# Staging the first-stage weights in eight places, and moving the token weights' two halves to other points of the queues

## The chip, the cores and the metric

The kernel runs on one core of a Trainium2 chip. The metric is the device time of one execution in microseconds (us), smaller is better. A core has five engines with queues of their own that run in order: TensorE (PE in the profile, with PEld for the loads of its stationary operand), VectorE (DVE), ScalarE (ACT), GpSimd (POOL) and SyncE (SP), which here issues every DMA.

## The reference, cut to what matters

Three layers follow one another, for 4 batches of 576 positions. The part that matters here is the first two:

```python
# layer 1: 8 heads of 64, four with a local band of 32 positions, four with stride 32
attn = softmax(mask(q @ k.T / 8)) @ v              # joined over the heads: x, 576 x 512
# layer 2
theta = x @ w_theta
zr, zi = x * cos(theta), x * sin(theta)
y = einsum('ts,bsd->btd', w_tok_r, zr) + einsum('ts,bsd->btd', w_tok_i, zi)
u = x + y
x = u + maximum(u @ w_ch, 0)
# layer 3: a gate picks 2 of 4 experts for each position; each expert is a causal
# attention of width 64 with projections wq, wk, wv, wo
```

w_theta, w_tok_r, w_tok_i and w_ch (w_theta 512 x 512, w_tok 576 x 576, w_ch 512 x 512) reach the chip as 64-bit floating-point numbers and are turned into 32-bit ones on the core.

## The kernel before, in words

Every product is made of three matmuls (`mm3`): each operand is split into a high and a low part, and high by high, high by low and low by high are summed in PSUM.

**Weights.** `load64` brings in a 64-bit weight in pieces of 128 rows by 256 or 288 columns. A piece is one DMA from SP (line 131) into a place of raw storage in `X[3]`, which is free so early; a cast on ACT of the top 16 bits (line 135); a shift and or on DVE (line 136), which ends the use of the place; and the split into a high part on ACT (line 102) and a low part on DVE (line 104, or line 106 where a scale is applied). `wth` (the angles' weights) has 8 pieces, `wtk` (the tokens' weights) two halves of 9 pieces, `wch` 8 pieces. There are four places; piece c uses place c % 4. The casts' results lie in `X[2]`, also four in number.

**The batches.** `attn_pair(b, pair)` computes one pair of heads of the first layer in three groups: scores into a PSUM tile `s`, exponentials on ACT, sums and reciprocals on DVE, a product with the reciprocal on POOL (line 212), transposes into `tp` (line 215), a copy `pt` (line 219), the product with the values into `av` (line 238), and a copy into `X[b]` (lines 243 and 245). `theta(b, h)` splits `X[b]` (`split_x`, only for h = 0), then forms the angles of one half of the channels in five tiles `th`, reduces them on DVE (lines 283, 284) and takes cosine and sine on ACT (lines 285, 297, 298). `rotate(b, h)` transposes `X[b]` into `xn` (line 305), multiplies it with cosine and sine on DVE (lines 315, 321, 322) and splits the result z (line 327 on ACT or 325; line 329). `tokens(b, h)` multiplies z with `wtk`, the first half of the output positions (n = 0) and then the second (n = 1), and adds into `X[b]` (line 344); `channels(b)` is the product with `wch`.

**The order.** A list scheduler orders each engine's queue from the program's order (which is the priority) and from modelled times; an instruction that is ready in its model may stand before one that comes earlier in the program. `issue_after(ins)` queues each instruction of a block behind `ins` on `ins`'s engine, and only there. For batch 0 the program has: the pairs 0 and 1, `wth`, the pairs 2 and 3; `theta(0, 0)`; the loads of batch 1's pair 0; `rotate(0, 0)`; the first half of `wtk`; `theta(0, 1)`; `rotate(0, 1)`; the second half of `wtk`; batch 1's pairs 0 and 1; `tokens(0, 0)`; `wch`; batch 1's pairs 2 and 3; `tokens(0, 1)`. While the first batch's attention runs (pool `ps0`), and from `theta(0, 0)` on (pool `ps1`), all eight PSUM banks are dealt out: in `ps1` two `acc` (for `th`, `y` and the channels' product), one `xn`, two `s`, one `t`, two `av`.

Of the kernel before, what the change touches and what calls it, by code (L numbers as in the profile page):

```python
# [12 lines left out]
F32 = mybir.dt.float32  # L13
F32R = mybir.dt.float32r
U32 = mybir.dt.uint32
U16 = mybir.dt.uint16
# [3 lines left out]
ALU = mybir.AluOpType  # L20
# [3 lines left out]
B, S, DM, HD, NE = 4, 576, 512, 64, 4  # L24
NT = 5
TW = [128, 128, 128, 128, 64]
HALF = S // 2
# [7 lines left out]
BLK = S // 32  # L35
# [12 lines left out]
def fused_kernel(ctx: ExitStack, tc: tile.TileContext, ql, kl, vl, qs, ks, vs, wth, wtk, wch, wqk, wvg, wo, out):  # L48
    nc = tc.nc

    def f(ap):
        return ap.bitcast(F32)
# [4 lines left out]
    X = [xpool.tile([128, 4, S], F32, name=f"X{b}") for b in range(B)]  # L57
# [27 lines left out]
    for rw in (LQ, RQ):  # L85
        t = wb.tile([128, 2, rw], BF16, name=f"twice{rw}")
# [30 lines left out]
    def new_split(pool, kt, n, name):  # L117
        return tuple(pool.tile([128, kt, n], F32R, name=f"{name}_{part}") for part in ("hi", "lo"))

    def load64(dst, src, kt, n0, n1, scale=1.0):  # L120

        hi, lo = dst
        n = n1 - n0
        for c in range(kt):
            raw = X[3].bitcast(U16)[:, c % 4, :4 * n]
            st = X[2][:, c % 4, HALF:HALF + n]  # L130
            nc.sync.dma_start(raw[:, :4 * n - 1], src[:, c, n0:n1].bitcast(U16)[:, 1:])
            mid = raw.bitcast(U32).rearrange("p (n t) -> p n t", t=2)[:, :, 0]
            top = raw.bitcast(BF16).rearrange("p (n t) -> p n t", t=4)[:, :, 2]
            head = X[2][:, c % 4, :n]
            got = nc.scalar.copy(head.bitcast(F16).rearrange("p (n t) -> p n t", t=2)[:, :, 1], top)
            nc.vector.scalar_tensor_tensor(st.bitcast(U32), mid, 13, head.bitcast(U32), op0=ALU.logical_shift_right,
                                           op1=ALU.bitwise_or)
            split_w(hi[:, c, n0:n1], lo[:, c, n0:n1], st, scale, nc.vector)
        return got.ins
# [2 lines left out]

        return b == 0 and pair != 2 or b == 1 and g == 0

    ps_of, loaded = {}, {}

    def load_pair(b, pair, ain, qbufs, kbufs):
        local = pair < 2
# [78 lines left out]
    def values(b, pair, part, xo, turned):  # L227
        local = pair < 2
        rw, kw = (LQ, LK) if local else (RQ, RQ)
        r0 = part[0][0]  # L230
        av = ps_of[b].tile([128, 512], F32, tag="av", bufs=2, name=f"av_{b}_{pair}_{r0}")
        with tc.issue_after(turned.ins) if b else nullcontext():
            for j0, pt, wd, vg in part:
                for i, wi in enumerate(wd):
                    w = kw if local else wi
                    c0 = rw * (j0 - r0 + i)
                    for h in range(2):
                        nc.tensor.matmul(av[64 * h:64 * h + 64, c0:c0 + wi], vg[:w, i, h, :], pt[:w, i, h, :wi],  # L238
                                         start=True, stop=True)
        c = sum(sum(wd) for _, _, wd, _ in part)  # L240
        copy = nc.scalar.copy if b == 0 else nc.vector.tensor_copy
        if local:
            copy(xo[:, rw * r0:rw * r0 + c], av[:, :c])
        else:
            copy(xo.rearrange("p (t r) -> p r t", r=32)[:, 3 * r0:3 * r0 + c // BLK, :],
                 av[:, :c].rearrange("p (r t) -> p r t", t=BLK))

    def split_act(x, name):
        hi = act.tile([128, S], F32R, tag="ahi", name=f"{name}_hi")
        lo = act.tile([128, S], F32R, tag="alo", name=f"{name}_lo")  # L250
        if len(xsplit) == B:
            nc.scalar.copy(hi, x)
        else:
            nc.vector.tensor_copy(hi, x)  # L254
        eng = nc.vector if not xsplit or len(xsplit) == B and name.endswith(("0", "2")) else nc.gpsimd
        eng.tensor_tensor(lo, x, f(hi), op=ALU.subtract)  # L256
        return hi, lo

    def mm3(ps, ahi, alo, bhi, blo, first, last):
# [7 lines left out]
    sins, turns = {}, {}  # L267
    xsplit, trig, z = {}, {}, {}

    def theta(b, h):  # L270
        if h == 0:
            xsplit[b] = split_x(b)
        xs = xsplit[b]
        d0 = 256 * h
        for t in range(NT):
            w, t0 = TW[t], 128 * t
            th = ps1.tile([128, 512], F32, tag="acc", bufs=2, name=f"th_{b}_{h}_{t}")
            for c in range(4):
                turned = mm3(th[:w, :256], xs[c][0][:, t0:t0 + w], xs[c][1][:, t0:t0 + w],
                             wth_hi[:, c, d0:d0 + 256], wth_lo[:, c, d0:d0 + 256], c == 0, c == 3)  # L280
            cs = rp.tile([128, 2, 256], F32, tag="cs", name=f"cs_{b}_{h}_{t}")
            r = cs[:w, 1, :]
            nc.vector.tensor_scalar_add(r, th[:w, :256], MAGIC)
            nc.vector.scalar_tensor_tensor(r, r, MAGIC, th[:w, :256], op0=ALU.subtract, op1=ALU.subtract)  # L284
            last = nc.scalar.activation(cs[:w, 0, :], r, AF.Abs)
            trig[h, t] = cs
            if b == 0:
                sines(b, h, range(t, t + 1))
        if b > 0:
            with tc.issue_after(last.ins):  # L290
                sines(b, h, range(NT))
        return turned.ins
# [7 lines left out]
    def rotate(b, h):  # L300
        for t in range(NT):
            w, t0, cs = TW[t], 128 * t, trig[h, t]
            xn = ps1.tile([128, 512], F32, tag="xn", bufs=1, name=f"xn_{b}_{h}_{t}")
            for c in range(2):
                nc.tensor.transpose(xn[:w, 128 * c:128 * c + 128], X[b][:, 2 * h + c, t0:t0 + w], ident)
            if t < 4:
                zf = cs
                if h == 0:
                    hi = zu.tile([128, S], F32R, tag="zuhi", name=f"zhi_{b}_{h}_{t}")
                    lo = zu.tile([128, S], F32R, tag="zulo", name=f"zlo_{b}_{h}_{t}")  # L310
                else:
                    hi = z1.tile([128, 512], F32R, tag=f"zhi{t}", name=f"zhi_{b}_{h}_{t}")
                    lo = z1.tile([128, 512], F32R, tag=f"zlo{t}", name=f"zlo_{b}_{h}_{t}")
                hi, lo = (v[:, :512].rearrange("p (a c) -> p a c", a=2) for v in (hi, lo))
                nc.vector.tensor_tensor(zf, cs, xn[:, None, :256].to_broadcast([128, 2, 256]), op=ALU.mult)
                z[h, t], z[h, 4 + t] = (hi[:, 0, :], lo[:, 0, :]), (hi[:, 1, :], lo[:, 1, :])
            else:
                zf = cs[:, 0, :]
                hi = zu.tile([128, 256], F32R, tag="z8hi", bufs=2, name=f"zhi_{b}_{h}_{t}")
                lo = zu.tile([128, 256], F32R, tag="z8lo", bufs=2, name=f"zlo_{b}_{h}_{t}")  # L320
                nc.vector.tensor_tensor(zf[0:64], xn[:64, :256], cs[:64, 0, :], op=ALU.mult)
                nc.vector.tensor_tensor(zf[64:128], xn[:64, :256], cs[:64, 1, :], op=ALU.mult)
                z[h, 8] = (hi, lo)
            if t % 2 == 0 and b > 0:
                nc.vector.tensor_copy(hi, zf)  # L325
            else:
                turns[b, h] = nc.scalar.copy(hi, zf).ins
            eng = nc.gpsimd if b > 0 else nc.vector
            eng.tensor_tensor(lo, zf, f(hi), op=ALU.subtract)  # L329

    us = {}

# [65 lines left out]

    for b in range(B):
        theta(b, 0)  # L400
        if b > 0:
            next_pair(b, 0)
            channels(b - 1)
        else:
            load_pair(1, 0, ain, 2, 2)
        rotate(b, 0)
        if b > 0:
            next_pair(b, 1)
        else:
            load64(wtk_s, wtk, 9, 0, HALF)  # L410
        turned = theta(b, 1)
        if b > 0:
            next_pair(b, 2)
        rotate(b, 1)
        if b == 0:
            load64(wtk_s, wtk, 9, HALF, S)
        if b == B - 1:
            with tc.issue_after(turns[b, 1]):
                nc.scalar.activation(spark, halfpi, AF.Exp)
            pha.close()  # L420
            wc = ctx.enter_context(tc.tile_pool(name="wc", bufs=1, side="right"))
            with tc.tile_pool(name="ws", bufs=3, side="right") as ws:
                with tc.issue_after(turns[b, 1]):
                    wqk_hi, wqk_lo = load_split(wc, ws, wqk, 4, 512, "wqk")
                    wvg_hi, wvg_lo = load_split(wc, ws, wvg, 4, 260, "wvg")
        if b == 0:
            with tc.issue_after(turned), tc.issue_after(sins[0, 1]):
                next_pair(b, 0)
                next_pair(b, 1)
        tokens(b, 0)  # L430
        if b == 0:
            with tc.issue_after(sins[0, 1]):
                for n0 in range(0, DM, 256):
                    load64(wch_s, wch, 4, n0, n0 + 256)
            next_pair(b, 2)
        next_pair(b, 3)
        tokens(b, 1)
# [347 lines left out]
```

## Time and profile before

| what | value |
|---|---|
| median of three runs | 566.6 us (565.12 to 568.58) |
| the profiled execution, its own time | 568.04 us |
| its span in the profile | 566.1 us |
| PE busy, share of the span | 531.6 us, 94% |
| DVE busy | 400.9 us, 71% |
| ACT busy | 317.3 us, 56% |
| POOL busy | 194.8 us, 34% |

The profile shows one execution. Its time is 1.9 us above its span, and 1.4 us above the median of the runs. Busy shares are averages over stages with different limits; the edit concerns the first 140 us.

### The profile page before, as it was taken

Reading aid. Unit: us, or ns where it says so; the run is one execution under the profiler, and the core shown is the slowest. Engines: PE = TensorE matmul, PEld = TensorE weight load, DVE = VectorE, ACT = ScalarE, POOL = GpSimd, SP = SyncE. Lnnn points to the kernel's source line nnn. Section 1 sums busy time; section 2 is a strip of 40 time slices with the busy share of each in tenths; the row PEclk is TensorE's granted clock in tenths of the full one; section 3 lists DMA queues with packets and bytes.
Section 4 is the critical chain, followed back from the end, with each engine's and each line's share of the span. In section 5 each row is a group of like instructions: output and inputs, shape, how many; then the busy total and the mean of one; then the engine's idle time right before and its main releaser. Section 6 shows DMA issues by size and latency. Waiting matters only on the chain.

```text
span 566.1 us, 12493 instructions
## 1 busy us (share of the span) xinstructions
PE 531.6 (94%) x4536; PEld 507.1 (90%) x4536; DVE 400.9 (71%) x1210; ACT 317.3 (56%) x904; POOL 194.8 (34%) x285
## 2 busy tenths in 40 slices
PE   5876799999999999999999999998999999999987
PEld 4855699999899999999999999897989999999987
DVE  3686998576666566856357543588988898888972
ACT  3886894433635226272143450386778668867873
POOL 2210002331265101535104470364455533634451
PEclk9957999999999999999999999999999999999999
DMA  9759341434020213000100020100001001100012
GB/s 268 233 181 316 115 147 52 133 124 156 1 86 23 97 35 117 26 23 8 57 1 1 1 58 0 38 2 2 0 10 45 34 1 33 54 1 12 33 43 85
DMA packets 20389, 37.53 MB, mean 66 GB/s; under 512 B 2904, under 2 KB 12296, under 8 KB 20328
## 3 DMA queue, kind: packets, MB, share of 16 engines
q1 hardware_dynamic: 20328, 36.73, 20.5%
q8 instruction: 36, 0.59, 0.4%
q14 instruction: 25, 0.20, 0.1%
HBM read 32.01 MB, written 4.72 MB: 65 GB/s over the span
## 4 chain that ended last, share of the span: by engine, by line
PE 69%; DVE 14%; DMA 8%; ACT 7%; issue 2%; POOL 1%; SPq 0%; DVEq 0%; POOLq 0%; ACTq 0%
PE y L260 7%; PE y L261 7%; PE y L262 7%; PE s L185 4%; PE th L260 3%; PE av L238 3%; DMA X<-in_wtk 3%; PE th L262 3%; PE th L261 3%; PE tp L617 3%; PE g L260 3%; PE g L261 3%; PE g L262 3%; DVE nm L596 2%; PE tp L215 2%; PE s L591 2%
## 5 line engine op out<-in xcount | busy, mean ns | idle before, releaser
L260 PE MATMUL y<-wtk_hi,zhi 128*128 128x288 f32 x288 | 86.3, 300 | 0.4 <-DVE X L344 0.4
L262 PE MATMUL y<-wtk_hi,zlo 128*128 128x288 f32 x288 | 85.6, 298 | 0.0
L261 PE MATMUL y<-wtk_lo,zhi 128*128 128x288 f32 x288 | 85.6, 297 | 0.0
L212 POOL TENSOR_TENSOR p<-p,sm 128x288 f32<-128x288 f32 (+2 forms) x48 | 28.7, 603 | 157.2 <-DVE sm L211 118.6
L614 POOL TENSOR_SCALAR p<-p,sm,gt 128x256 f32<-128x256 f32 (+1 forms) x64 | 45.2, 710 | 52.1 <-DVE sm L612 34.0
L607 ACT ACTIVATE p<-s,nm 128x128 f32<-128x128 f32 (+2 forms) x96 | 49.5, 518 | 15.0 <-DVE nm L596 7.9
L260 PEld LDWEIGHTS y<-wtk_hi,zhi 128*128 128x128 f32 x288 | 54.1, 188 | 0.7 <-DVE X L344 0.7
L329 POOL TENSOR_TENSOR zlo<-cs,zhi 128x512 fp32r<-128x512 f32 (+1 forms) x30 | 35.8, 1206 | 54.0 <-DVE zhi L325 43.3
L261 PEld LDWEIGHTS y<-wtk_lo,zhi 128*128 128x128 f32 x288 | 54.1, 188 | 0.1
L262 PEld LDWEIGHTS y<-wtk_hi,zlo 128*128 128x128 f32 x288 | 54.0, 188 | 0.1
L260 PE MATMUL th<-wth_hi,x_hi 128*128 128x256 f32 (+1 forms) x160 | 48.1, 301 | 4.9 <-DVE cs L284 3.4
L596 DVE TENSOR_REDUCE nm<-s 128x1 f32<-128x128 f32 (+2 forms) x96 | 44.2, 468 | 5.3 <-PE s L594 4.4
L185 PE MATMUL s<-k,q 128*108 128x54 f32 (+2 forms) x320 | 43.1, 277 | 3.3 <-DMA k<-in_kl 3.3
L261 PE MATMUL th<-wth_lo,x_hi 128*128 128x256 f32 (+1 forms) x160 | 45.9, 288 | 0.0
L262 PE MATMUL th<-wth_hi,x_lo 128*128 128x256 f32 (+1 forms) x160 | 45.7, 289 | 0.0
L185 PEld LDWEIGHTS s<-k,q 128*108 128x108 f32 (+1 forms) x320 | 41.2, 199 | 4.2 <-issue 4.0
L219 ACT COPY pt<-tp 96x384 f32<-96x384 f32 (+2 forms) x44 | 20.9, 477 | 40.8 <-PE tp L215 40.6
L256 POOL TENSOR_TENSOR x_lo<-X,x_hi 128x576 fp32r<-128x576 f32 x20 | 29.8, 1492 | 32.7 <-DVE x_hi L254 26.4
L260 PE MATMUL pq<-x_hi,wqk_hi 128*128 128x288 f32 x128 | 39.8, 311 | 1.0 <-DVE q L542 0.8
L260 PE MATMUL g<-u_hi,wch_hi 128*128 128x288 f32 x128 | 38.7, 303 | 1.4 <-DVE X L366 1.4
L626 DVE TENSOR_TENSOR ptlo<-tp,pthi 128x128 fp32r<-128x128 f32 (+4 forms) x80 | 37.6, 478 | 1.2 <-ACT pthi L625 0.6
L261 PE MATMUL pq<-x_lo,wqk_hi 128*128 128x288 f32 x128 | 38.0, 297 | 0.0
(172 smaller groups left out, 1697.8 us busy)
## 6 DMA issues: line engine op xcount, KB each, us to landing
X<-in_wtk SPq DMA_DIRECT2D x18, 287.8 KB
q<-in_qs SPq DMA_DIRECT2D x8, 594.0 KB
q<-in_ql SPq DMA_DIRECT2D x8, 576.0 KB
v<-in_vl SPq DMA_DIRECT2D x24, 144.0 KB
out_t<-X SPq DMA_DIRECT2D x20, 128.0 KB
k<-in_kl SPq DMA_DIRECT2D x8, 304.0 KB
k<-in_ks SPq DMA_DIRECT2D x8, 288.0 KB
X<-in_wth SPq DMA_DIRECT2D x8, 255.8 KB
```

The lines of the kernel that those rows point to most:

```text
L185: nc.tensor.matmul(s[:rm, i * kw:i * kw + w], qt[:, j0 + i, :], kt[:, k0:k0 + w], start=False, stop=i == n - 1)
L212: nc.gpsimd.tensor_tensor(tiles(p), tiles(p), each(sm), op=ALU.mult)
L219: copy(pt[:kw, :n * rm], tp[:kw, :n * rm])
L256: eng.tensor_tensor(lo, x, f(hi), op=ALU.subtract)
L260: nc.tensor.matmul(ps, ahi, bhi, start=first, stop=False)
L261: nc.tensor.matmul(ps, ahi, blo, start=False, stop=False)
L262: return nc.tensor.matmul(ps, alo, bhi, start=False, stop=last)
L329: eng.tensor_tensor(lo, zf, f(hi), op=ALU.subtract)
L596: nc.vector.tensor_reduce(nm[:w, t + ci:t + ci + 1], s[:w, :c1 - c0], axis=AX.X, op=ALU.max, negate=True)
L607: nc.scalar.activation(p[:w, c0:c1], scs[ci][:w, :c1 - c0], AF.Exp, bias=nm[:w, t:t + 1], scale=1.0, accum_out=acc)
L614: eng.tensor_scalar(p[:w, :kn], p[:w, :kn], sm[:w, t:t + 1], gt[:w, t, e:e + 1], op0=ALU.mult, op1=ALU.mult)
L626: nc.vector.tensor_tensor(dst(ptlo), src, f(dst(pthi)), op=ALU.subtract)
```

## The change: what it does

`load64` takes its place of raw storage from a running count of pieces. The pieces of `wth` and `wtk` go in turn to `X[1]` and `X[3]`, four places in each, so eight in all; those of `wch` (`late=True`) use the four places of `X[3]` only, since `X[1]` takes the results of batch 1 by then. The casts' results stay in four places of `X[2]`.

The first half of `wtk` moves up in the program, ahead of `rotate(0, 0)`, to where the loads of batch 1's pair 0 were; its ACT instructions are queued behind the last copy of batch 0's values, its DVE instructions behind the last split of `X[0]`. The loads of batch 1's pair 0 come with that pair itself, after both halves of `wtk`. The second half of `wtk` stays where it was, with its ACT instructions behind the last copy of z of the first half of the channels and its DVE instructions behind the last subtraction of it.

In batch 0, `th` tiles of odd number take the PSUM banks of tag `s` and two of three `xn` tiles those of tag `av`.

```diff
-    def load64(dst, src, kt, n0, n1, scale=1.0):
+    pieces = []
+
+    def load64(dst, src, kt, n0, n1, scale=1.0, late=False):
...
-            raw = X[3].bitcast(U16)[:, c % 4, :4 * n]
+            place = X[3] if late or len(pieces) % 2 else X[1]
+            raw = place.bitcast(U16)[:, len(pieces) // (1 if late else 2) % 4, :4 * n]
+            pieces.append(c)
...
-            copy(xo[:, rw * r0:rw * r0 + c], av[:, :c])
+            valued[b] = copy(xo[:, rw * r0:rw * r0 + c], av[:, :c]).ins
...
-        eng.tensor_tensor(lo, x, f(hi), op=ALU.subtract)
+        halved[name] = eng.tensor_tensor(lo, x, f(hi), op=ALU.subtract).ins
...
-            th = ps1.tile([128, 512], F32, tag="acc", bufs=2, name=f"th_{b}_{h}_{t}")
+            th = ps1.tile([128, 512], F32, tag="s" if b == 0 and t % 2 else "acc", bufs=2, name=f"th_{b}_{h}_{t}")
...
-            xn = ps1.tile([128, 512], F32, tag="xn", bufs=1, name=f"xn_{b}_{h}_{t}")
+            tag, bufs = ("av", 2) if b == 0 and t % 3 else ("xn", 1)
+            xn = ps1.tile([128, 512], F32, tag=tag, bufs=bufs, name=f"xn_{b}_{h}_{t}")
...
-            eng.tensor_tensor(lo, zf, f(hi), op=ALU.subtract)
+            halved[b, h] = eng.tensor_tensor(lo, zf, f(hi), op=ALU.subtract).ins
...
-            load_pair(1, 0, ain, 2, 2)
+            with tc.issue_after(valued[0]), tc.issue_after(halved["x0_0_3"]):
+                load64(wtk_s, wtk, 9, 0, HALF)
         rotate(b, 0)
         if b > 0:
             next_pair(b, 1)
-        else:
-            load64(wtk_s, wtk, 9, 0, HALF)
...
         if b == 0:
-            load64(wtk_s, wtk, 9, HALF, S)
+            with tc.issue_after(turns[0, 0]), tc.issue_after(halved[0, 0]):
+                load64(wtk_s, wtk, 9, HALF, S)
...
-                    load64(wch_s, wch, 4, n0, n0 + 256)
+                    load64(wch_s, wch, 4, n0, n0 + 256, late=True)
```

## Rows read from the trace of the kernel before

**Rows 1.** Busy time of each engine in five stretches of the first 133 us

```profile
25.00:47.00 22.00, 14.77 (x153) 11.59 (x152) 19.63 (x56) 19.14 (x73) 2.62 (x5) 0.57 0.70 216
47.00:73.84 26.84, 19.39 (x143) 17.14 (x142) 21.84 (x54) 20.80 (x52) 0.00 (x0) 0.97 0.58 183
73.84:91.70 17.86, 17.86 (x142) 17.70 (x141) 16.52 (x46) 13.62 (x44) 2.06 (x3) 1.00 0.32 110
91.70:100.00 8.30, 8.30 (x94) 7.71 (x92) 6.24 (x18) 3.19 (x9) 1.61 (x3) 1.00 0.39 129
100.00:133.00 33.00, 32.42 (x379) 30.71 (x378) 22.01 (x66) 12.42 (x39) 11.15 (x14) 1.00 0.45 144
```

**Rows 2.** Chain that ended last, 28 to 60 us: start, us, what

```profile
31.77 5.29 DMA X<-in_wtk
...
46.48 7.25 DMA X<-in_wtk
```

**Rows 3.** ACT's groups by form, 30 to 47 us: busy us, mean ns, idle before

```profile
L135 ACT CAST X<-X 128x288 f16<-128x288 bf16 x11 | 5.5, 517 | 2.9 <-DMA X<-in_wtk 2.9
```

**Rows 4.** Timeline of ACT: start, us, line, what

```profile
37.09 0.52 ACT L135 CAST X<-X 128x288 f16<-128x288 bf16 x1 [1.03 <-DMA X<-in_wtk]
37.47 0.29 ACT L202 ACTIVATE p<-s,mx 108x54 f32<-108x54 f32 x1
...
42.22 0.41 ACT L219 COPY pt<-tp 54x324 f32<-54x324 f32 x1
...
44.50 0.39 ACT L245 COPY X<-av 128x144 f32<-128x144 f32 x1
```

**Rows 5.** Timeline of POOL, the last group of batch 0's attention

```profile
39.46 0.49 POOL L212 TENSOR_TENSOR p<-p,sm 108x162 f32<-108x162 f32 x1 [2.10 <-DVE sm L211]
```

**Rows 6.** Timeline of PE, 40 to 74 us

```profile
40.00 0.74 PE L215 MATMUL tp<-ident,p 108*54 108x108 f32 x3 [0.29 <-POOL p L212]
...
42.68 0.86 PE L238 MATMUL av<-pt,v 54*64 54x54 f32 x12 [0.75 <-ACT pt L219]
44.95 0.58 PE L260 MATMUL th<-wth_hi,x_hi 128*128 128x256 f32 x1 [1.41 <-ACT X L245]
...
48.52 0.33 PE L261 MATMUL th<-wth_lo,x_hi 128*128 128x256 f32 x1
...
72.17 0.30 PE L181 MATMUL s<-mask_l,twice 128*128 128x288 bf16 x1
...
73.84 0.38 PE L260 MATMUL y<-wtk_hi,zhi 128*128 128x288 f32 x1
```

**Rows 7.** Timeline of DVE, 45 to 74 us: start, us, line, what

```profile
45.04 0.45 DVE L254 CAST x_hi<-X 128x576 fp32r<-128x576 f32 x1
...
46.26 0.75 DVE L256 TENSOR_TENSOR x_lo<-X,x_hi 128x576 fp32r<-128x576 f32 x1
...
54.34 0.46 DVE L136 SCALAR_TENSOR_TENSOR X<-X,X 128x288 uint32<-128x288 uint32 x1 [3.11 <-ACT X L135]
...
61.26 0.68 DVE L329 TENSOR_TENSOR zlo<-cs,zhi 128x512 fp32r<-128x512 f32 x1
61.86 0.67 DVE L315 TENSOR_TENSOR cs<-cs,xn 128x512 f32<-128x512 f32 x1
62.46 0.44 DVE L136 SCALAR_TENSOR_TENSOR X<-X,X 128x288 uint32<-128x288 uint32 x1
62.83 0.41 DVE L284 SCALAR_TENSOR_TENSOR cs<-cs,th 64x256 f32<-64x256 f32 x1
63.16 0.44 DVE L104 TENSOR_TENSOR wtk_lo<-X,wtk_hi 128x288 fp32r<-128x288 f32 x1
...
69.94 0.42 DVE L329 TENSOR_TENSOR zlo<-cs,zhi 128x256 fp32r<-128x256 f32 x1
...
73.17 0.67 DVE L329 TENSOR_TENSOR zlo<-cs,zhi 128x512 fp32r<-128x512 f32 x1
```

More of the change, by code (lines that the diff above doesn't have):

```diff
@@ L143, in per_tile @@
         return b == 0 and pair != 2 or b == 1 and g == 0
-    ps_of, loaded = {}, {}
+    ps_of, loaded, valued, halved = {}, {}, {}, {}
     def load_pair(b, pair, ain, qbufs, kbufs):
@@ L242, in values @@
         if local:
-            copy(xo[:, rw * r0:rw * r0 + c], av[:, :c])
+            valued[b] = copy(xo[:, rw * r0:rw * r0 + c], av[:, :c]).ins
         else:
-            copy(xo.rearrange("p (t r) -> p r t", r=32)[:, 3 * r0:3 * r0 + c // BLK, :],
-                 av[:, :c].rearrange("p (r t) -> p r t", t=BLK))
+            valued[b] = copy(xo.rearrange("p (t r) -> p r t", r=32)[:, 3 * r0:3 * r0 + c // BLK, :],
+                             av[:, :c].rearrange("p (r t) -> p r t", t=BLK)).ins
     def split_act(x, name):
```

## The prediction, made before the changed kernel was run

> **What bounds the kernel now.** I read the busy times by stretch first, then the chain of waits, then the timelines of the engines that the chain names. By stretch [rows 1], the early part has two regimes. From 73.84 us on PE is full: 17.86 of 17.86, 8.30 of 8.30, 32.42 of 33.00 us. There only the moment at which PE gets going, and what starves it later, can move the end. From 25 to 73.84 us PE is busy 14.77 of 22.00 and 19.39 of 26.84 us, so 14.7 us of it are idle, and its granted clock is 0.57 in the first of the two (mostly the 1.2 GHz level). DVE and ACT are what is nearly full there: DVE has 2.4 and 5.0 us to spare, ACT 2.9 and 6.0. So before 73.84 us the two elementwise engines carry the time, and even behind it DVE has only 1.3 us to spare in 17.86.
>
> The chain shows what breaks them up: twice it hangs on a piece of the token weights, 5.29 us from 31.77 and 7.25 us from 46.48 [rows 2]. ACT takes its queue in order, so a cast whose DMA has not landed holds all that stands behind it: 2.9 us in front of the casts between 30 and 47 us [rows 3]. At 54.34 DVE has waited 3.11 us for such a cast [rows 7]; the sines of the first two angle tiles were queued behind it too. The DMA behind the second of these was slow because the loads of batch 1's pair 0, which the program has earlier, stood ahead of it on SP.
>
> **The change, part by part.** All times below are on the profiled execution's clock (568.04 us, of which 566.1 is the span); the difference is then taken off the median, which is 1.4 us lower.
>
> *First half of wtk behind batch 0's values.* In the stretch to 47 us, 11 casts of wtk (5.5 us, and 2.9 us of waits for their DMAs) stand among batch 0's exponentials and copies on ACT [rows 3]. Four of them lie ahead of the last exponential at 37.47, the last with a DMA wait of 1.03 us [rows 4]; with 0.38 from the start of the cast to that of the exponential behind it, they make 4 x 0.38 + 1.03, some 2.5 us, so that exponential would end near 35.2 in place of 37.7. From there I add up the last group's way with nothing in between: sum and reciprocal on DVE 0.4 (an estimate, two instructions on a few columns), POOL 0.49 [rows 5], transposes 0.74 [rows 6], copy 0.41 [rows 4], values 0.86 [rows 6], copy into X 0.39 [rows 4], split 0.45 and 0.75 [rows 7], and 1.0 for eight hand-overs of about 0.12: 5.5 us, so the split of X[0] ends at about 40.7 instead of 47.0 [rows 7]. The gain is 6.3 us. If only the part ahead of the last exponential is gained, it is 2.5. I take 6.3, since ACT and DVE, the engines that made each of the later steps wait, then have nothing else queued; theta starts near 39.5 in place of 44.95 [rows 6].
>
> *What then must be done before the first token product.* DVE is the longer engine, and I price its work by the distances between starts in a full stretch [rows 7]: line 329 0.60, line 315 0.60, line 136 0.37, line 284 0.33 (line 283 taken as equal, and the low part as line 136, which is as long: 0.44). A piece of wtk is 0.37 + 0.37 = 0.74; nine are 6.7 us. One half of the channels is five tiles of 0.33 + 0.33 + 0.60 + 0.60 = 1.87: 9.3 us. Of the other half, the two reductions of each tile (3.3 us) also fall before y, since they free the PSUM banks that PE's queue needs. From 40.7: 6.7 + 9.3 + 3.3 = 19.3, so 60.0; with 1 us for waits on the first angles, z of the first half is complete at 61. Before, that was 69.94 + 0.42 = 70.36 [rows 7], and y began 3.5 us later at 73.84 [rows 6], behind two angle tiles and two score groups. I allow 2: y begins at 63, 10.8 us earlier.
>
> *What is owed.* By 73.84 the kernel before had all 18 pieces behind it, and of the second half of the channels two line 315 and two line 329 (the second at 73.17, [rows 7]). The new one has nine pieces (6.7) and these four (2.4) still to do on DVE when PE gets going: 9.1 us. In the 26.16 us behind 73.84, DVE has 1.34 + 2.06 = 3.4 us to spare, and 11.0 in the 33 behind those [rows 1]. So 5.7 us of the debt can't be paid within 26 us. At worst PE stalls for all of that; at best for none, because the token products need little from DVE and the eight pieces of wch (8 x 0.74 = 5.9 us) could wait until 133. I take 4.8, near the worst, because in the stretch to 91.70 PE and DVE are both full already, and attention needs DVE at every step.
>
> *The other edits.* The eight places let the last four pieces of wth be issued at once; ACT is full from 25 on, so this gains between 0 and 1 us, and I count 0. They also take batch 1's loads out of the way of the second DMA wait, whose 3.11 us of idle DVE is inside the sum above. Staging in X[1] costs nothing: batch 1's first values come behind its first scores, exponentials and transposes, and so behind the last piece that is read there. The extra banks for th and xn remove waits of PE alone, which is not the bound there; that the score tiles then wait for an angle tile to be reduced costs 0 to 0.4, I take 0. The loads of pair 0 move behind wtk on SP. If they stand behind its last piece, whose place comes free only after z of the first half (61.4), 1.3 MB follow (576, 304 and three times 144 KB); 216 GB/s at a DMA share of 0.70 [rows 1] are some 300 at a full one, by which they need 4.4 us, and land near 67. PE has y of the first positions until 70, so this costs nothing at once, but it holds batch 1's attention (first scores at 72.17 before, [rows 6]) to a lead of 5 us. The price is 0 to 5.8 of the 10.8 us, and overlaps with the debt; I don't add it.
>
> Sum: 10.8 - 4.8 = 6.0 us earlier, with ends of 1.3 (the split gains only 2.5, and the debt costs all of it) and 10.8. That is 562.0 for the profiled execution and 560.6 for the median. A measurement of this kernel can tell about 1% from no change, that is 5.7 us; the forecast lies on that border.
>
> **The rivals.**
>
> The debt is paid for nothing (A): wch and the attention give way, and y keeps PE full. For it: DVE has 11 us to spare behind 100 us [rows 1]. Against it: the program's order puts wch ahead of batch 1's later pairs. Then 10.8 us earlier, 555.8.
>
> DVE's work is conserved (B): what is not done under batch 0's attention must be done by 91.70 all the same. Nine pieces that lay ahead of 47 us, 6.7 us, come behind the split; the idle time of DVE from there to 91.70 is 5.0 + 1.3 = 6.3 us [rows 1], of which I leave 3.0 for waits that stay. So 3.4 of the 6.7 are not covered, and of the 6.3 us by which the split ends earlier 2.9 are left: 563.7. For it: DVE is 92% busy from 73.84 to 91.70, with attention work that can't wait for long.
>
> Slower (C): the tail of batch 0's attention does not shorten, since its last group is a chain through POOL, PE and ACT whose hand-overs may be what takes the time. The split then ends at 47.0 as before, with nine pieces more behind it: by B's sum the state of 91.70 is reached 3.4 us later, at 570.0; where the late loads hold batch 1's attention as well, up to 574. The point from which it decides is a split that ends later than 47.0 - 3.4 = 43.6. Against it: the copies of that tail were taken up late by ACT, which had casts in front of them (transposes end at 40.74, [rows 6], their copy begins at 42.22, [rows 4]).
>
> The clock falls again (D): y now comes behind a longer stretch in which PE waits for DVE, and starts at 1.2 GHz. For it: from 25 to 47 us the granted clock is 0.57 though PE is busy two thirds of the time [rows 1], and theta's matmuls start slow at 44.95 and grow shorter only at 48.52 [rows 6]. Against it: from 47 to 73.84 it stayed at 0.97 with a PE that was idle for 28% of the time [rows 1]. A rise took 48.52 - 44.95 = 3.6 us, of which 1.8 are lost at half speed: 562.4. The Trainium skill, "TensorE: Matmul & The Clock Gate", section "What's actually happening", says that the low level is the default and that activity releases it; by that the gaps before y would speak for D, and the sum would be 562.4 instead of 560.6. The rows from 47 us on show a clock that holds through gaps of the size I expect, so I leave D a small chance.
>
> The queues don't change much (E): the scheduler already had this order in the main, and the time stays, 566.6. Rows 2 speak against it.
>
> **How the numbers follow.** The forecast has 0.37, A 0.19, B 0.18, C 0.14, D 0.06, E 0.06. Predicted time 560.6. Its own ends are 555.8 and 565.3. For eight in ten the range runs from 554 (A, with 1 us from the places of wth and the scatter of the runs) to 570 (C's nearer end), which leaves out most of C and a little of A. Faster by over 1% (below 560.9) are A and some two thirds of the forecast's cases: 0.44. Slower by over 1% (above 572.3) is about half of C and a little for what I have not thought of: 0.09. Within 1%: 0.47.
>
> **What would show it.** In the changed kernel's profile the last split of X[0] should end near 41 us, no cast should wait for a wtk DMA before the angles, the last line 329 of the first half should lie near 61, and the first y matmul near 63. The debt shows as idle PE, or as DVE over 95% busy, between 63 and 95. The prediction is wrong if the split still ends past 43, if y begins early but batch 1's last values come no earlier, or if PE's saturated stretch has gaps of more than 5 us.

## The result, and the profile after

The changed kernel takes 560.33 us (median of four runs, 559.4 to 563.35), the kernel before 567.59 us beside it: a ratio of 0.989, with a 95% interval of 0.986 to 0.993. That is 6.1 us, with an interval of some 4.0 to 8.2. The forecast was 560.6.

The profiled execution took 563.35 us with a span of 561.5; the four runs' spans lie between 557.6 and 561.5. So the marks inside the trace tell more than the end does. I use four of them:

- the end of the last split of X[0] (lines 256 and 260),
- the end of the last subtraction of z of the first half of the channels ("z"),
- the start of the first token product ("y"),
- the first load of the sine table for batch 1 on ACT ("the load"); from it to the same load of the last batch the two kernels run at one distance (140.40 to 290.35 and 132.03 to 281.97), so what is gained at the load was gained ahead of it and is still there in the last batch.

Busy times by stretch after (columns as in [rows 1]: PE, PEld, DVE, ACT, POOL, granted clock, DMA share, GB/s):

```profile
25.00:47.00 22.00, 16.53 (x162) 14.42 (x161) 15.23 (x42) 14.07 (x52) 6.04 (x4) 0.69 0.58 181
47.00:73.84 26.84, 21.94 (x173) 20.64 (x172) 24.73 (x59) 25.60 (x68) 0.00 (x0) 1.00 0.42 144
73.84:91.70 17.86, 17.02 (x150) 16.15 (x151) 17.86 (x54) 12.06 (x39) 3.25 (x4) 1.00 0.48 147
100.00:133.00 33.00, 32.92 (x391) 31.01 (x389) 22.68 (x67) 12.51 (x33) 8.59 (x11) 1.00 0.48 157
```

Against [rows 1], DVE and ACT do less up to 47 us (19.63 to 15.23 and 19.14 to 14.07) and more from 47 to 73.84 (21.84 to 24.73 and 20.80 to 25.60); from 73.84 to 91.70 DVE has no gap. The marks, from DVE's timeline after (they answer to [rows 7]):

```profile
39.91 0.76 DVE L260 TENSOR_TENSOR x_lo<-X,x_hi 128x576 fp32r<-128x576 f32 x1
...
47.73 0.46 DVE L140 SCALAR_TENSOR_TENSOR X<-X,X 128x288 uint32<-128x288 uint32 x1 [1.23 <-ACT X L139]
...
61.57 0.42 DVE L334 TENSOR_TENSOR zlo<-cs,zhi 128x256 fp32r<-128x256 f32 x1
61.91 0.45 DVE L140 SCALAR_TENSOR_TENSOR X<-X,X 128x288 uint32<-128x288 uint32 x1
```

from PE's (they answer to [rows 6]):

```profile
39.44 0.58 PE L264 MATMUL th<-wth_hi,x_hi 128*128 128x256 f32 x1 [0.50 <-ACT X L249]
...
61.80 0.37 PE L264 MATMUL y<-wtk_hi,zhi 128*128 128x288 f32 x1
```

and from ACT's, after and then before:

```profile
47.19 0.51 ACT L139 CAST X<-X 128x288 f16<-128x288 bf16 x1 [2.48 <-DMA X<-in_wtk]
...
132.03 1.28 ACT L301 ACT_TABLE_LOAD   x1
```

```profile
140.40 1.28 ACT L297 ACT_TABLE_LOAD   x1
```

The split ends at 40.67 instead of 47.01 (6.3 us earlier), z at 61.99 instead of 70.36 (8.4), y starts at 61.80 instead of 73.84 (12.0), and the load at 132.03 instead of 140.40 (8.4). The first piece of the second half (line 140 at 61.91) stands right behind z. One thing is not as foreseen: ACT still waits 2.48 us for a DMA of wtk, the ninth piece.

A part of these differences is not the change's. In the one profiled execution of the kernel before, the first loads came late, ahead of anything that the change touches: its first load of k took 5.53 us, against 4.27 to 4.63 in the six other kernels whose chain of waits has it. The first piece of `wth` on SP and the first copy of values on ACT, before and then after:

```profile
13.25 5.03 SPq L131 DMA_DIRECT2D X<-in_wth  x4
```

```profile
19.96 0.32 ACT L243 COPY X<-av 128x192 f32<-128x192 f32 x1
```

```profile
11.37 6.31 SPq L135 DMA_DIRECT2D X<-in_wth  x8
```

```profile
17.71 0.32 ACT L247 COPY X<-av 128x192 f32<-128x192 f32 x1
```

In the twelve other kernels below, the first piece of `wth` is issued between 11.03 and 12.05 us and that copy starts between 16.81 and 17.97. Five of them have four places, and the same order on SP up to there as the kernel before. So some 2 us of every difference from the marks before belong to this late start. Of the 8.4 us at the load some 6.5 are left for the change, and of the 12.0 at y some 10. (Both are estimates; the issue of `wth` is 1.9 us apart. The ratios below give much the same: over the thirteen kernels they are worth 1.8 us less, on average, than what the load shows.) Differences between kernels other than the one before carry no such step, but their own starts are up to 1 us apart.

Why is the span only 4.6 us shorter when the load is 8.4 us earlier? In the third layer, which the change does not touch, the granted clock of the profiled execution falls for one stretch. The same stretch, after (8.4 us earlier on its own clock, by the lead so far), and before:

```profile
371.60:391.60 20.00, 17.90 (x118) 16.62 (x118) 16.02 (x48) 12.23 (x36) 9.35 (x14) 0.83 0.00 1
```

```profile
380.00:400.00 20.00, 17.79 (x139) 16.54 (x138) 18.31 (x60) 13.83 (x41) 10.16 (x16) 1.00 0.01 1
```

With PE just as busy it gets through 118 matmuls instead of 139. By the next marks, the outputs of batch 0 (421.34 before, 415.56 after), the lead is 5.8 us. A second, shorter fall follows near the end (0.57 from 547.40 to 551.40 us, where the kernel before has 1.00 from 552 to 560). The other three runs after, at 557.6 to 559.2 us of span, have granted clocks of 0.984 to 0.986 instead of 0.979.

### The profile page after: what moved, and what is told of

The parts are those of the page before. It is cut to its first block, busy times and chain, and to the rows that moved or that the text cites. A ratio compares the mean times of both kernels' runs of the same rounds, so it can differ in the third digit from the quotient of the medians.

```text
span 561.5 us, 12501 instructions
## 1 busy us (share of the span) xinstructions
PE 532.7 (95%) x4536; PEld 509.5 (91%) x4536; DVE 398.9 (71%) x1210; ACT 316.3 (56%) x904; POOL 199.2 (35%) x285
## 4 chain that ended last, share of the span: by engine, by line
PE 68%; DVE 15%; ACT 6%; POOL 2%; issue 2%; DMA 2%; DVEq 0%; POOLq 0%; ACTq 0%
PE y L264 6%; PE y L266 6%; PE y L265 6%; PE av L242 4%; PE s L189 3%; PE th L264 3%; PE th L266 3%; PE g L264 3%; PE tp L622 3%; PE g L266 3%; PE g L265 3%; PE th L265 3%; PE tp L219 2%; DVE nm L601 2%; PE o L578 2%
## 5 line engine op out<-in xcount | busy, mean ns | idle before, releaser
L216 POOL TENSOR_TENSOR p<-p,sm 128x288 f32<-128x288 f32 (+2 forms) x48 | 33.3, 700 | 144.2 <-DVE sm L215 57.8
L619 POOL TENSOR_SCALAR p<-p,sm,gt 128x256 f32<-128x256 f32 (+1 forms) x64 | 45.2, 709 | 53.7 <-DVE sm L617 35.2
```

The lines of the kernel that those rows point to most:

```text
L216: nc.gpsimd.tensor_tensor(tiles(p), tiles(p), each(sm), op=ALU.mult)
L619: eng.tensor_scalar(p[:w, :kn], p[:w, :kn], sm[:w, t:t + 1], gt[:w, t, e:e + 1], op0=ALU.mult, op1=ALU.mult)
```

## The experiments

Each kernel was run four to ten times beside the kernel before, once with a profile. This table has the marks of all, as read from that one trace (us), and the ratio of the times with its interval. The marks in the row "before" carry the late start; the ratios compare many executions.

| kernel | split | z | y | load | ratio to before |
|---|---|---|---|---|---|
| before | 47.01 | 70.36 | 73.84 | 140.40 | 1 |
| changed | 40.67 | 61.99 | 61.80 | 132.03 | 0.989 (0.986 to 0.993) |
| changed, first half free | 45.14 | 62.44 | 64.59 | 132.65 | 0.988 (0.984 to 0.993) |
| changed, second half free | 40.43 | 67.94 | 68.11 | 138.53 | 1.000 (0.997 to 1.004) |
| changed, banks as before | 40.93 | 63.19 | 67.37 | 134.02 | 0.988 (0.984 to 0.992) |
| changed, four places | 38.61 | 60.45 | 62.00 | 133.50 | 0.995 (0.993 to 0.998) |
| before, second half behind z | 43.51 | 61.86 | 66.63 | 135.89 | 0.995 (0.991 to 0.998) |
| before, first half moved | 39.60 | 66.53 | 71.03 | 137.47 | 0.997 (0.994 to 1.000) |
| before, eight places | 50.15 | 66.76 | 70.96 | 137.46 | 1.000 (0.997 to 1.004) |
| before, second half and banks | 43.64 | 61.04 | 61.89 | 134.12 | 0.989 (0.985 to 0.993) |
| changed, second half later still | 40.34 | 60.67 | 60.48 | 133.48 | 0.989 (0.986 to 0.993) |
| changed, batch 1's loads behind the ninth piece | 40.49 | 60.23 | 60.04 | 130.24 | 0.984 (0.980 to 0.989) |
| the same, product on DVE | 38.14 | 56.52 | 58.44 | 126.15 | 0.981 (0.976 to 0.987) |
| before, product on DVE | 43.61 | 68.14 | 71.63 | 138.22 | 1.000 (0.996 to 1.004) |

**The first half no longer queued**

```diff
-            with tc.issue_after(valued[0]), tc.issue_after(halved["x0_0_3"]):
-                load64(wtk_s, wtk, 9, 0, HALF)
+            load64(wtk_s, wtk, 9, 0, HALF)
```

> The changed kernel, but the first half of wtk is no longer queued behind batch 0's values and split (it keeps its new place in the program, the eight places and all the rest). Marks read from the traces: the last split of X[0] ends at 47.0 us before and 40.7 after, the first token product begins at 73.84 and 61.80, the first sine table load of batch 1 at 140.40 and 132.03. My theory, that the casts and shifts of wtk among batch 0's last steps cost the 6.3 us: the split ends past 44 again, the table load comes at 135 to 139, 3 to 7 us are lost, some 564 to 567 us. The rival, that eight places bring the DMAs early enough for those casts to cost nothing: the split stays near 41 and the time near 560.

The split went back by 4.5 us, as my theory has it, and the load by 0.6 only, which neither theory had; the ratio is the changed kernel's too. Two lines of DVE's timeline in this kernel and one of ACT's say it:

```profile
44.38 0.76 DVE L260 TENSOR_TENSOR x_lo<-X,x_hi 128x576 fp32r<-128x576 f32 x1
...
62.03 0.41 DVE L334 TENSOR_TENSOR zlo<-cs,zhi 128x256 fp32r<-128x256 f32 x1
```

```profile
132.65 1.28 ACT L301 ACT_TABLE_LOAD   x1
```

The nine pieces take the same time on DVE ahead of the split or behind it (28.36 us of work from 25 us to the end of z, against 28.17 in the changed kernel), and z ends within half a microsecond of where it did. The early split is a fact, but on top of the other parts it is worth next to nothing.

**The second half no longer queued**

```diff
-            with tc.issue_after(turns[0, 0]), tc.issue_after(halved[0, 0]):
-                load64(wtk_s, wtk, 9, HALF, S)
+            load64(wtk_s, wtk, 9, HALF, S)
```

> The changed kernel, but the second half of wtk is no longer queued behind z of the first half of the channels. My theory: the split still ends at 40.7; pieces of the second half go in between, z of the first half (last line 334 at 61.6 us after) comes 2 to 6 us later and so does the first token product; the debt of DVE is smaller by as much, so that only 1 to 3 us of the 8.4 are lost at the table load (133 to 135), some 561 to 563 us. The rival, that this wait is what makes the gain: all 8 us are lost, 567 or more. Another rival, that the scheduler had this order anyway: nothing moves, 132.0.

The split stays and 6.5 us go at the load. With the late start taken off the 8.4, that is the whole gain, and the ratio of 1.000 and the median of 568.1 us say the same: the rival was right, and my theory (1 to 3) wrong. DVE's busy time from 25 us to the end of z, before, changed, and in this kernel (each stretch ends where its z does; the third busy figure is DVE's):

```profile
25.00:70.36 45.36, 30.72 (x265) 25.61 (x264) 37.99 (x100) 36.82 (x116) 2.62 (x5) 0.77 0.67 207
```

```profile
25.00:61.99 36.99, 28.22 (x256) 25.37 (x255) 28.17 (x73) 27.86 (x86) 6.04 (x4) 0.82 0.54 182
```

```profile
25.00:67.94 42.94, 30.11 (x253) 26.09 (x251) 34.26 (x89) 33.48 (x102) 6.05 (x4) 0.78 0.55 187
```

DVE's idle time in them is 7.4, 8.8 and 8.7 us: the changed kernel has no less of it. What is smaller is the work ahead of z, 28.17 us against 37.99 and 34.26. In DVE's timeline 17 low parts of wtk stand ahead of the end of z before and in this kernel, nine in the changed one; the eight more at 0.74 us a piece are 5.9 us, and this kernel has 6.1 us more than the changed one. (The kernel before has 3.7 us more than this one, most of it by its late start: up to 25 us its DVE was busy for 11.43 us, here for 14.64.) A part of the loss may be the clock's: it was granted at 0.87 from 47 to 73.84 us here (1.00 in the changed kernel), and the first token products ran at the lower level.

**The banks as before**

```diff
-            th = ps1.tile([128, 512], F32, tag="s" if b == 0 and t % 2 else "acc", ...)
+            th = ps1.tile([128, 512], F32, tag="acc", ...)
...
-            tag, bufs = ("av", 2) if b == 0 and t % 3 else ("xn", 1)
+            tag, bufs = "xn", 1
```

> The changed kernel with the angle tiles in two banks and the transposes in one, as before. My theory, that PE is not the bound before the token products and these banks remove waits of PE alone: 0 to 1 us lost at the table load (132 to 133), 560 to 561 us. The rival, that theta held up by its two banks delays the angles and so DVE and ACT: 3 us or more, the first token product at 65 or later, 563 us or more.

2.0 us are lost at the load, between the two; y at 67.37 is later than the rival's 65. z is only 1.2 us later, but y no longer follows it at once: 4.2 us lie between them, as 3.5 did before. PE still has angle tiles of the second half and two score groups to do then. The ratio of the times does not resolve this.

**Four places**

```diff
-            place = X[3] if late or len(pieces) % 2 else X[1]
-            raw = place.bitcast(U16)[:, len(pieces) // (1 if late else 2) % 4, :4 * n]
+            raw = X[3].bitcast(U16)[:, c % 4, :4 * n]
```

> The changed kernel with four places of raw storage as before. My theory: the split of X[0] still ends near 41; but five of the nine pieces of the first half now get their place only when an earlier one is shifted, from 41 us on, and land 2 to 6 us later, so ACT waits for DMAs in the stretch from 41 to 52; 2 to 5 us of the 8.4 are lost (table load at 134 to 137), 562 to 565 us. The rival, that the places make the whole gain: all of it is lost, 567. The other rival, that the queueing alone makes it: 132 and 560.

1.5 us are lost at the load, a little less than I expected, with waits of ACT for a DMA of wtk of up to 3.58 us. By the ratios the loss is 3.5 us, though their intervals touch. The split is 2 us earlier than with eight places; see the last section.

**The second half alone, on the kernel before**

```diff
-            load64(wtk_s, wtk, 9, HALF, S)
+            with tc.issue_after(turns[0, 0]), tc.issue_after(halved[0, 0]):
+                load64(wtk_s, wtk, 9, HALF, S)
```

> The kernel before with one part of the change alone: the second half of wtk queued behind z of the first half of the channels. Theory now (after the four kernels that undo one part each): what counts is that DVE and ACT reach z of the first half without nine pieces in between, and the pieces themselves cost the same earlier or later. It expects the split of X[0] to end at 47 as before, the first token product at 66 to 69 instead of 73.84, the first sine table load of batch 1 at 134 to 137 instead of 140.40, 561 to 564 us. The rival, that this order only pays when the first half is out of the attention's tail too: 139 or later, 565 or more.

As the new theory had it: z at 61.86, y at 66.63, the load 4.5 us earlier. Without the late start some 2.5 us of these are left, and the ratio gives 3.0. The split moved to 43.51, which I had not expected: the scheduler ordered the attention's tail anew.

**The first half alone, on the kernel before**

```diff
+            with tc.issue_after(valued[0]), tc.issue_after(halved["x0_0_3"]):
+                load64(wtk_s, wtk, 9, 0, HALF)
         rotate(b, 0)
...
-        else:
-            load64(wtk_s, wtk, 9, 0, HALF)
```

> The kernel before with another part alone: the first half of wtk at its new place and queued behind batch 0's values and split, four places, batch 1's first loads behind it, second half free. The theory of the prediction, that an early split is worth its 6 us: split at 39 to 41, table load at 134 to 136, 561 to 563 us. The theory now, that the nine pieces only change places with the work behind them: split at 39 to 41 as well, but the first token product at 71 to 75 and the table load at 138 to 142, 564 to 568 us.

The split is at 39.60, even earlier than in the changed kernel, yet y starts at 71.03 and the load comes at 137.47, 2.9 us earlier. Without the late start that is about 1 us, and the ratio gives 1.6 (0 to 3.2): next to nothing is left of the prediction's step, as the new theory had it. Here z has 13 low parts ahead of it instead of 17.

**Eight places alone, on the kernel before**

```diff
-            raw = X[3].bitcast(U16)[:, c % 4, :4 * n]
+            place = X[3] if late or len(pieces) % 2 else X[1]
+            raw = place.bitcast(U16)[:, len(pieces) // (1 if late else 2) % 4, :4 * n]
+            pieces.append(c)
```

> The kernel before with the eight places alone. The theory now: DMAs land earlier, ACT's waits for them shrink (5.7 us in all from 25 to 75 us before), but DVE's work in front of the first token product is the same; table load at 138 to 141 (0 to 2 us gained). The rival, that ACT's waits for DMAs are the bound: 4 us or more gained, 136 or earlier.

The load is 2.9 us earlier, with the latest split of all (50.15; two of POOL's products are held in this kernel, see the last section) and with no wait of ACT for a DMA of wtk between 30 and 75 us. Without the late start about 1 us is left, as I expected, and the time shows none of it (ratio 1.000, 0.997 to 1.004). The rival falls: ACT's waits are gone and 4 us were not gained.

**Batch 1's loads behind the ninth piece, on the changed kernel**

```diff
-            nc.sync.dma_start(raw[:, :4 * n - 1], ...)
+            brought[0] = nc.sync.dma_start(raw[:, :4 * n - 1], ...).ins
...
             with tc.issue_after(valued[0]), tc.issue_after(halved["x0_0_3"]):
                 load64(wtk_s, wtk, 9, 0, HALF)
+            with tc.issue_after(brought[0]):
+                load_pair(1, 0, ain, 2, 2)
```

> The changed kernel with the loads of batch 1's pair 0 queued on SP behind the DMA of the ninth piece of wtk, which in the changed kernel stands behind them, lands 5.7 us after its issue and holds ACT for 2.48 us at 47.19. If that wait is on the path: it goes, DVE's idle 1.23 us in front of it too, z of the first half ends 1 to 2.5 us earlier than 61.99, table load at 129.5 to 131. If DVE's other work fills the gap anyway: 132.0, no change. If batch 1's attention misses its loads: later than 132.5.

SP's issues, in the changed kernel and then in this one:

```profile
39.09 0.33 SPq L161 DMA_DIRECT2D q<-in_ql  x1
39.47 0.42 SPq L162 DMA_DIRECT2D k<-in_kl  x1
39.94 1.36 SPq L166 DMA_DIRECT2D v<-in_vl  x3
41.40 1.97 SPq L135 DMA_DIRECT2D X<-in_wtk  x4
```

```profile
40.89 0.33 SPq L135 DMA_DIRECT2D X<-in_wtk  x1
41.32 0.37 SPq L161 DMA_DIRECT2D q<-in_ql  x1
...
43.67 6.22 SPq L135 DMA_DIRECT2D X<-in_wtk  x8
```

The changed kernel's chain of waits shows what the order cost, and ACT's timeline here what became of it:

```profile
41.40 5.71 DMA X<-in_wtk
```

```profile
130.24 1.28 ACT L301 ACT_TABLE_LOAD   x1
```

The wait of 2.48 us is gone, z is 1.8 us earlier and so is the load, while the split is only 0.2 earlier. This wait was on the path. The ratio of 0.984 is better than the changed kernel's 0.989, but their intervals overlap.

**Second half and banks, on the kernel before**: the second half's edit above, and the two lines of the change for `th` and `xn`.

> The kernel before with two parts of the change: the second half of wtk behind z of the first half of the channels, and the more banks for the angle tiles and transposes. The second half alone gave 4.5 us at the first sine table load of batch 1 (135.89 against 140.40) and left y 4.8 us behind z (66.63 against 61.86). If the banks are what lets y follow z at once, y begins near 62 to 63 and the load comes at 133.5 to 135, 560 to 563 us. If they only matter with the eight places, 135.5 to 136.5.

y at 61.89, 0.9 us behind z, and the load at 134.12, 1.8 us earlier than with the second half alone. Two of the four parts bring 6.3 of the 8.4 us (without the late start some 4.5 of 6.5), and by the ratio all of it (0.989). So the banks' worth is not bound to the eight places.

**The second half later still**

```diff
-            with tc.issue_after(turns[0, 0]), tc.issue_after(halved[0, 0]):
+            with tc.issue_after(turns[0, 1]), tc.issue_after(halved[0, 1]):
```

> The changed kernel with the second half of wtk queued even later, behind z of the second half of the channels (last line 334 at 76.55 us after). It puts a price on the debt of the prediction: 6.7 us of DVE's work then stand behind 70 us, and the second positions' product on PE waits for them. If the debt has to be paid by PE as the prediction took it: PE idle by 3 to 7 us between 65 and 85, table load at 134 to 138, 562 to 566 us. If PE has other work (batch 1's scores, transposes, attention): 131.5 to 133, 559 to 561.

The load comes at 133.48, 1.5 us later than in the changed kernel, between the two expectations; the ratio is the same. y is 1.3 us earlier, and it is given back where PE's timeline has its waits for the second half:

```profile
71.47 0.53 PE L264 MATMUL y<-wtk_hi,zhi 128*128 128x288 f32 x2 [1.09 <-ACT wtk_hi L102]
73.67 0.61 PE L265 MATMUL y<-wtk_lo,zhi 128*128 128x288 f32 x1 [1.34 <-DVE wtk_lo L104]
```

**The product on DVE**, on the kernel with batch 1's loads behind the ninth piece:

```diff
-            nc.gpsimd.tensor_tensor(tiles(p), tiles(p), each(sm), op=ALU.mult)
+            eng = nc.vector if b == 0 and pair > 1 else nc.gpsimd
+            eng.tensor_tensor(tiles(p), tiles(p), each(sm), op=ALU.mult)
```

> The kernel with batch 1's first loads behind the ninth piece (table load at 130.24, split of X[0] at 40.49), and for batch 0's pairs 2 and 3 the product with the reciprocal (line 216) on DVE instead of POOL. With the eight places one of these products took 3.76 us on POOL instead of 0.46 to 0.58, while DVE was busy without a gap. If that hold is what keeps the split at 40: no 3 us step is left, the split ends at 36 to 38.5, DVE's idle time before z shrinks by 1.5 to 3 us, and the load comes at 127.5 to 129.5. If the tail's length is set elsewhere: the split at 39.5 to 41 and the load at 130 to 131.5, since DVE has some 2 us more to do.

The split ends at 38.14 and the load comes at 126.15, 4.1 us earlier than without this edit (more than the 0.7 to 2.7 expected) and 14.3 earlier than before, some 2 of them the late start. At a median of 556.79 us and a ratio of 0.981 (0.976 to 0.987) it is the fastest of all, though its interval overlaps with that of the kernel it is built on, and by the ratios the step between the two is 1.6 us.

**The same edit alone, on the kernel before**

> The kernel before with one edit alone: for batch 0's pairs 2 and 3 the product with the reciprocal on DVE instead of POOL. In the kernel before POOL took 0.46 to 0.58 us for each of these products, and none was held. If the 4.1 us that this edit gave on top of the eight places came from the hold: little here, table load at 139 to 141.5 (140.40 before), 565.5 to 568 us. If they came from two hand-overs less per group: 136 to 138, 561.5 to 564 us.

The load comes at 138.22, 2.2 us earlier, just past the end of what the hand-overs would give (136 to 138). But about as much is the late start, and the time shows nothing gained: a median of 567.17 us and a ratio of 1.000 (0.996 to 1.004), as expected if the 4.1 us came from the hold. The hand-overs alone don't make them. How much of the 4.1 us is the hold itself stays open, since the edit also lets the scheduler order the tail anew.

## Why the prediction came out right, step by step

*The time.* Forecast 6.0 us, measured 6.1 by the ratio, and some 6.5 at the load without the late start. The two large terms came out near: y some 10 us earlier (put at 10.8), of which 3.7 are given back by the load (put at 4.8). That the sum meets the time to 0.1 us is luck all the same, and the interval of some 4 to 8 us could not tell it from 5 or 7. Two terms that it put at nothing go against one another: the banks brought 2.0 us and the wait for the ninth piece cost 1.8.

*First half behind batch 0's values.* The split was put at 40.7 and ends at 40.67; theta was put at 39.5 and starts at 39.44. Both are luck: the last exponential ended at 33.3 rather than 35.2, which is the 2 us by which this execution started earlier, and the way from it took 7.4 us rather than 5.5, since from 34.66 to 38.96 PE made the transposes and values of the last two groups one after the other. (In the chain of waits one of POOL's products, held for 3.76 us, lies ahead of this; see the last section.) The queueing is worth 4.5 us at the split, not 6.3. And **the weight given to this step failed**: the prediction called it a gain of 6.3 us, more than half of its 10.8. Taking the queueing away costs 0.6 us at the load. Rival B's rule, that DVE's work is conserved, holds for this half even more than B had it (2.9 us left). B's time of 563.7 failed because it did not count what the second half's queueing takes out from ahead of z.

*Work ahead of z.* The sum of 19.3 us was right in its size (z at 61.99 against 61), because it counted nine pieces of wtk and not eighteen. That is the second half's wait, which the prediction counted without naming it as a term. Shown by the experiments: without it the ratio is 1.000 and 6.5 us are lost at the load, and alone it brings 3.0 us by the ratio.

*The banks.* Costed at nothing, since PE was not the bound ahead of y. They are worth 2.0 us at the load: without them y stands behind angle tiles of the second half and two score groups, 4.2 us behind z. The step "I allow 2" between z and y was the right place, and measured 0.2 before the end of z.

*The debt.* 3.7 us of the early y are given back by the load (put at 4.8); the late start lies ahead of this stretch and is not in it. From y to the load, before and after:

```profile
73.84:140.40 66.56, 65.98 (x680) 63.39 (x679) 49.24 (x140) 31.31 (x96) 14.82 (x19) 1.00 0.39 128
```

```profile
61.80:132.03 70.23, 67.71 (x684) 64.13 (x683) 57.31 (x164) 39.21 (x119) 15.39 (x19) 1.00 0.45 141
```

DVE has 8.1 us more to do in this stretch (57.31 against 49.24; the debt was put at 9.1). Of the 3.67 us, 1.94 are PE standing idle (2.52 against 0.58), and 1.73 more busy time of PE. One score group that stood ahead of y before makes some 0.9 of that, two transposes fewer take 0.3 off, and the rest is not accounted for. The prediction took all of its 4.8 for stalls. Rival A (the debt paid for nothing) falls; so does C, since the split is early. Deferring still more, behind z of the second half, gives back more than it gains at the marks: y is 1.3 us earlier and the load 1.5 later.

*The DMAs.* "No cast should wait for a wtk DMA before the angles" was wrong: one waits 2.48 us at 47.19. The scheduler put batch 1's loads not behind wtk on SP, as the program has them, but ahead of the ninth piece, whose place was not free. It cost 1.8 us.

*The clock.* D did not happen ahead of y: the granted clock is 1.00 from 47 to 73.84 us. It fell in the third layer of the profiled execution instead, which no rival had.

*What stays open.* Why the loads of the one execution before came late, why marks and ratios still differ by some 2 us for single kernels (four places: some 5 us left at the load, 2.6 by the ratio), and the share of POOL's hold in the last edit.

## What to carry to other kernels

Where the length of a stretch follows the work of its fullest engine, moving work inside it changes the marks and not the end: ask of each piece of work whether the next engine needs it before it can start, and queue behind that point only what is not needed yet. Read the gain of a part at a mark behind the whole stretch, and undo parts one by one; the part that moved its own mark most was worth least here. Before you trust a difference between marks, compare the first microseconds of the two traces, ahead of anything that was changed: the one trace of the kernel before had started late, and every difference from it was some 2 us too large. A load that the program's order puts late can still be issued early when the queue ahead of it is waiting for a place, so look at the issuing queue itself.

## What the runs showed of the hardware that I had not expected

A product on POOL can take many times its usual length while DVE is busy without a gap. POOL's timeline in the changed kernel, two products of a kind that took 0.46 to 0.58 us each before (one of them in [rows 5]); then the chain of waits, which has the first of them alone:

```profile
26.72 4.26 POOL L216 TENSOR_TENSOR p<-p,sm 108x162 f32<-108x162 f32 x2 [2.92 <-ACT X L247]
```

```profile
26.73 3.76 POOL p L216
```

DVE's timeline over the same time, the end of a stretch with no gap:

```profile
29.08 0.74 DVE L260 TENSOR_TENSOR x_lo<-X,x_hi 128x576 fp32r<-128x576 f32 x1
29.75 0.41 DVE L106 SCALAR_TENSOR_TENSOR wth_lo<-X,wth_hi 128x256 fp32r<-128x256 f32 x1
30.09 0.16 DVE L215 RECIPROCAL sm<-sm 108x4 f32<-108x4 f32 x1
32.57 0.43 DVE L106 SCALAR_TENSOR_TENSOR wth_lo<-X,wth_hi 128x256 fp32r<-128x256 f32 x1 [2.33 <-ACT wth_hi L102]
```

The product ends at 30.49, a quarter of a microsecond after DVE falls idle at 30.25. The seven kernels with eight places and this product on POOL all show it (4.26 to 5.43 us for the two), and with the eight places alone a later product is held as well, for 3.44 us from 40.63, until 0.3 us after DVE falls idle at 43.75. None of the five kernels with four places and this product on POOL shows it. There DVE has small gaps at this point, and the product of the same group took 0.46 us:

```profile
25.30 0.46 POOL L215 TENSOR_TENSOR p<-p,sm 108x162 f32<-108x162 f32 x1 [2.92 <-DVE sm L214]
```

The Trainium skill, "SBUF — State Buffer", section "Who interferes with whom", says that GpSimd's only read and write ports are a pair that it shares with VectorE, that an instruction of VectorE with two inputs from SBUF contends for it with an instruction of GpSimd that reads SBUF, and that the pair is an exclusive lock. The trace fits that: six of the ten instructions from 26.73 to 30.25 (lines 106, 140, 260) have two operands there. The other four (lines 214, 215, 223, 258) have one, and POOL did not get in at those either, which the sentence above does not cover. In the kernel before it went the other way round: a shift on DVE that usually takes 0.44 us [rows 7] took 0.78 while a product ran on POOL, DVE's and POOL's timeline:

```profile
33.50 0.78 DVE L136 SCALAR_TENSOR_TENSOR X<-X,X 128x288 uint32<-128x288 uint32 x1
```

```profile
33.41 0.55 POOL L212 TENSOR_TENSOR p<-p,sm 108x216 f32<-108x216 f32 x1 [3.16 <-DVE sm L211]
```

That it is this port, and not something else that ended with the stretch, was argued from the timelines and not tried by itself.

The second thing is the granted clock in the third layer: one fall to the lower level in one execution, 0.83 over 20 us (0.55 from 376.60 to 381.60, behind 5 us in which PE was busy for 3.86), went with a loss of 2.6 us of the lead (8.4 to 5.8). That is nearly half of what the change brings, in a part of the kernel that it leaves alone.
